# Windowed attention in front of two MoE layers: alternating the column halves in the value products, and one score path for all units

## The chip, the core and the metric

The kernel runs on one core of a Trainium2 chip. The metric is the device time of one execution in microseconds (us), the median of several runs. The engines are TensorE (PE; its weight loads are listed apart as PEld), VectorE (DVE), ScalarE (ACT), GpSimd (POOL) and the DMA queues, most of them issued from SyncE (SP).

## What is computed

Three stages follow each other, all in float32. The change lies in the first.

```
q, k, v: 4 x 8 heads x 576 x 64
scores = 0.125 * q @ k.T ; mask = (rel >= 0) & (rel < 64) ; attn = softmax(where(mask, scores, -1e9))
x  = attn @ v                                   # 2304 tokens x 512
x  = g(x @ w_in) @ w_out                        # 512 -> 2048 -> 512, g piecewise quadratic
out[n] = gate * (relu(x @ w1[e]) @ w2[e])       # e = argmax of x @ w_gate, 8 experts
```

## The kernel before

The 2304 tokens are 18 tiles of 128 rows. Attention is cut into 36 **units**: one tile and one half of the heads (4 heads). The first MoE layer goes over 7 **blocks** of 256 or 384 tokens in **steps**: one step is 12 matmuls of the first layer into `h` (L486, 256 or 384 columns), an activation on ACT and DVE (`a`, `ghi`, `glo`), and 6 or 9 matmuls of the second layer into `acc` (L528, 512 columns), two steps later. Float32 operands of these layers are split into a high part `hi` and a remainder `lo` and multiplied in a faster 32-bit format (fp32r), three products for one. Then follow 48 steps of the second MoE layer and the tokens left over.

A unit goes through these stages: scores into the PSUM tile `S` (`u_qk`), row maximum (`mask_parts`: `mx` on DVE, `nm` on ACT), exponential on ACT (`u_exp`), normalising (`norm_parts`), transposing (`tr_parts`: by PE into `pt`, from unit `DT0` = 24 on by a DMA transpose), copy to `pb`, products with the values (`av_parts`, L442), and a copy to the block's `xT` as hi and lo. The product with the values takes four heads and two blocks of 64 rows, so eight matmuls of 128 rows by 64 columns. In the trace each is two, as every plain float32 matmul there. `od`, the outermost of the three loops, chooses the half of the array's columns: the first four write output partitions 0 to 63, the last four 64 to 127.

There are two score paths. Units 0 to 14 (`NQ`) are multiplied in plain float32 on tiles of 64 rows by 64 columns, four at a time, and PE adds the mask first with small bf16 matmuls (L310, L316). Units 15 to 35 load twice as much (1280 instead of 640 elements a partition, zero-padded or doubled), `u_split` cuts it into hi and lo on ACT, DVE and POOL (L272 to L284), `u_scores` makes eight matmuls of 128 x 128 by 192 columns (L334), DVE adds the mask in two halves and writes the result to SBUF (L343), and the maximum is read from there (L373).

What sets the order: the first 10 units and the first 22 steps stand in a list written out by hand (`HEAD`). After it, `plan` gives each unit a start slot (two slots to a step) and `STAGES`, `STAGES2` (units 15 to 23) or `STAGES3` (from unit 24) say how many slots later each stage is recorded. A scheduler then places the recorded instructions on each engine by its own estimate of when they are ready; each engine runs its queue in that order. Raw inputs of units from 10 on go through one buffer (`RB` = 1), and the load of unit u+1 is issued behind `u_split(u)`.

Of the kernel before, what the change touches and what calls it, by code (L numbers as in the profile page):

```python
# [19 lines left out]
P = 128  # L20
# [25 lines left out]
ST3 = (-3, -1, 0, 1, 2, 6, 7)  # L46
US_A = (0, 3, 4, 5, 7, 11, 21)
UJ_V = ()
ST2 = (-2, -1, 0, 1, 3, 3, 4)
LEFT = (0, 0)  # L50
RB = 1
# [3 lines left out]
NQ = 15  # L55
MASK_PE = tuple(range(NQ))
# [28 lines left out]
QLO_V = (0, 2, 8, 10, 11, 20, 22, 31, 34, 35)  # L85
KLO_V = (0, 1, 3, 5, 8, 10, 11, 12, 22, 24, 31)
QHI_V = (0, 3, 4, 5, 7, 10, 11, 13, 16, 19, 23, 24, 28, 30, 31)
KHI_V = (1, 4, 5, 7, 8, 9, 10, 15, 20, 26, 29, 30, 32, 34, 35)
# [40 lines left out]
def kernel(  # L129
# [3 lines left out]
    qk: bass.AP,  # L133
# [104 lines left out]
    def u_load(u):  # L238
        if u < len(units):
            b, c, hf = units[u]  # L240
            if u < EARLY:
                r = wp.tile([P, 640], F32, tag="w", name="qqr")
            else:
                r = att.tile([P, 640 if u < NQ else 1280], F32, tag="qk", name="qk", bufs=RB)
            nc.sync.dma_start(r, qq[:, u] if u < NQ else qk[:, u - NQ])
            U.setdefault(u, {})["r"] = r
# [16 lines left out]
    def u_split(u):  # L263
        if u < NQ:
            return
        s = U[u]

        raw = s["r"]
        r = att.tile([P, 2048], F32R, tag="qs", name="qs", bufs=QB)
        q, k, kh = r[:, :512], r[:, 512:1280], r[:, 1280:]  # L270
        if u in QHI_V:
            nc.vector.tensor_copy(q, raw[:, :512])  # L272
        else:
            nc.scalar.activation(q, raw[:, :512], ACTF.Copy)  # L274
        if u in KHI_V:
            nc.vector.tensor_copy(kh, raw[:, 512:])  # L276
        else:
            nc.scalar.activation(kh, raw[:, 512:], ACTF.Copy)
        qeng = nc.vector if u in QLO_V else nc.gpsimd
        keng = nc.vector if u in KLO_V else nc.gpsimd  # L280
        qeng.tensor_tensor(  # L281
            out=q[64:], in0=raw[64:, :512], in1=q[64:].bitcast(F32), op=ALU.subtract
        )
        keng.tensor_tensor(out=k, in0=raw[:, 512:], in1=kh.bitcast(F32), op=ALU.subtract)  # L284
        s.update(qs=q, kk=r[:, 512:].rearrange("p (c h k) -> p h c k", c=2, h=4))

    def u_qk(u):
        s = U[u]
        S2 = None
        if u < min(ALT, NQ) and u % 2:  # L290
            S = [ps.tile([P, 512], F32, tag="acc", name="Sa", bufs=3) for _ in range(2)]
        else:
            S2 = ps.tile([P, 2, 512], F32, tag="S", name="S")
            S = [S2[:, a] for a in range(2)]
        s["S"], s["S2"] = S, S2
        if u < NQ:

            rq, rk = s["r"][:, :2 * P], s["r"][:, 2 * P:]

            pe = u in MASK_PE  # L300
            kind = mask_of(u)
            for pr in range(2):
                outs = [
                    (a, r, slice(64 * a, 64 * a + 64), S[a][64 * r:64 * r + 64, pr * P:pr * P + P])
                    for r in range(2) for a in range(2)
                ]
                if pe:
                    for a, r, rows, o in outs:
                        m = 1 + a if kind == 1 + r else 0
                        mm = nc.tensor.matmul(  # L310
                            o, ib[rows, 64 * a:64 * a + 64], mb[rows, m], start=True, stop=False
                        )
                        if u == BEHIND:
                            tc.keep_in_program_order(mm)
                for a, r, rows, o in outs:
                    nc.tensor.matmul(  # L316
                        o,
                        rq[rows, pr * P + 64 * r:pr * P + 64 * r + 64],
                        rk[rows, pr * 192 + 64 * r:pr * 192 + 64 * r + P],
                        start=not pe, stop=True,  # L320
                    )
            return
        s["sr"] = att.tile([P, 4, P], F32, tag="sr", name="sr", bufs=2)
        u_scores(u, S2)

    def u_scores(u, S2):

        s = U[u]
        sr = s["sr"]
        for a in range(2):  # L330
            for b in range(2):
                h = 2 * a + b
                for c in range(2):
                    nc.tensor.matmul(  # L334
                        S2[:, a, 192 * b:192 * b + 192], s["qs"][:, h * P:h * P + P],
                        s["kk"][:, h, c], start=(c == 0), stop=(c == 1),
                    )
        sv = S2[:, :, :384].rearrange("p a (b k) -> p a b k", b=2)
        so = sr.rearrange("p (a b) k -> p a b k", b=2)
        m = mb[:, mask_of(u)].unsqueeze(1).unsqueeze(1).to_broadcast([P, 2, 2, P])  # L340
        for r in range(2):
            rs, ks = slice(64 * r, 64 * r + 64), slice(64 * r, 64 * r + P)
            nc.vector.tensor_tensor(out=so[rs], in0=sv[rs, :, :, ks], in1=m[rs], op=ALU.add)  # L343

    def mask_parts(u):
        s = U[u]
        sr = s["sr"] if u >= NQ else att.tile([P, 4, P], F32, tag="sr", name="sr", bufs=2)
        mx = att.tile([P, 4], F32, tag="mx", name="mx", bufs=2)
        m = mb[:, mask_of(u)].unsqueeze(1)
        if u >= NQ:  # L350
            pass
        elif s["S2"] is not None:
            sv = s["S2"][:, :, :2 * P].rearrange("p a (b k) -> p a b k", b=2)
            if u in MASK_PE:
                nc.vector.tensor_reduce(
                    out=mx.rearrange("p (b a) -> p a b", a=2), in_=sv, axis=AX.X, op=ALU.max
                )
            else:
                nc.vector.tensor_tensor(
                    out=sr.rearrange("p (b a) k -> p a b k", a=2), in0=sv,  # L360
                    in1=m.unsqueeze(1).to_broadcast([P, 2, 2, P]), op=ALU.add,
                )
        else:
            for a in range(2):
                sv = s["S"][a][:, :2 * P].rearrange("p (b k) -> p b k", b=2)
                if u in MASK_PE:
                    nc.vector.tensor_reduce(out=mx[:, a::2], in_=sv, axis=AX.X, op=ALU.max)
                else:
                    nc.vector.tensor_tensor(
                        out=sr[:, a::2], in0=sv, in1=m.to_broadcast([P, 2, P]), op=ALU.add  # L370
                    )
        if u not in MASK_PE:
            nc.vector.tensor_reduce(out=mx, in_=sr, axis=AX.X, op=ALU.max)  # L373
        yield
        nm = att.tile([P, 4], F32, tag="nm", name="nm", bufs=2)
        nc.scalar.activation(nm, mx, ACTF.Copy, scale=-0.125)
        s.update(sr=sr, nm=nm)
# [3 lines left out]
    def u_exp(u):  # L381
# [3 lines left out]
        for h in range(4):  # L385
            nc.scalar.activation(
                sr[:, h], s["S"][h % 2][:, h // 2 * P:h // 2 * P + P] if u in MASK_PE else sr[:, h],
                ACTF.Exp, scale=0.125,
                bias=s["nm"][:, h:h + 1], accum_out=sm[:, h:h + 1],
            )  # L390
# [41 lines left out]
    def av_parts(u):  # L432
# [4 lines left out]
        for od in range(2):  # L437
            for pr in range(2):
                h = 2 * pr + od
                for blk in range(2):  # L440
                    cs = slice(64 * blk, 64 * blk + 64)
# [32 lines left out]
    STAGES = [(-2, u_split), (0, u_qk), (0, u_mask), (1, u_exp), (2, u_norm), (3, u_tr), (4, u_av)]  # L474
    hl = u_split, u_qk, u_mask, u_exp, u_norm, u_tr, u_av
    STAGES2, STAGES3 = list(zip(ST2, hl)), list(zip(ST3, hl))
# [448 lines left out]
    def plan(us, s0, s1):  # L925
        for i, u in enumerate(us):
            st = s0 + ((s1 - 6 - s0) * i) // max(1, len(us) - 1)
            for off, fn in STAGES if u < NQ else STAGES2 if u < DT0 else STAGES3:
                slots.setdefault(st + off, []).append((fn, (u,)))
# [83 lines left out]
    def run_slot(s):  # L1013
        for fn, a in slots.get(s, []):
            fn(*a)
            if fn is u_split and a[0] + RB >= EARLY:
                u_load(a[0] + RB)
# [43 lines left out]
    for x in HEAD:  # L1061
# [10 lines left out]
        if x == "av9":  # L1072
            u_load(10)
            v_load(10)
# [34 lines left out]
def layout(q, k, v, w_in, w_out, w_gate, w1, w2):  # L1109
# [7 lines left out]
    qq = np.zeros((P, NQ, 2 * P + 2 * 192), np.float32)  # L1117
    qk = np.zeros((P, 2 * NTILE - NQ, 4 * P + 4 * 192), np.float32)
    vv = np.zeros((P, NTILE, 2, 2, 4 * D), np.float32)
    for c in range(NTILE):  # L1120
        for hf in range(2):
# [4 lines left out]
            for r in range(2):  # L1126
                o = slice(D * r, D * r + D)
                if u < NQ:
                    qq[o, u, :2 * P] = a[:, r::2].reshape(D, 2 * P)
                    qq[o, u, 2 * P:] = b[:, r::2].reshape(D, 2 * 192)  # L1130
                else:
                    qk[o, u - NQ, :4 * P] = a.reshape(D, 4 * P)
                    qk[o, u - NQ, 4 * P:] = b.reshape(D, 4 * 192)
# [8 lines left out]
        "qq": qq, "qk": qk, "vv": vv, "wi": wi, "wo": wo, "wg": w_gate.T,  # L1142
# [27 lines left out]
```

## Time and profile before

| | |
|---|---|
| median of 3 runs | 745.62 us (745.48 to 746.74) |
| the profiled execution's own time | 744.77 us |
| its span, first to last instruction | 743.0 us |
| PE busy | 714.0 us (96%) |
| DVE, ACT, POOL busy | 488.7, 418.2, 144.5 us |

Busy times of PE count a matmul from its start to its modelled end, and matmuls overlap, so a busy PE can still be made faster. Starts of matmuls are the firmer numbers: the time between the start of one group and the start of the next is what the group costs the queue.

### The profile page before, as it was taken

The numbers are of one execution on the slowest core, as the hardware profiler recorded it, in microseconds if no ns is written. First come the engines' busy times: TensorE is split into PE (matmuls) and PEld (weight loads), VectorE is DVE, ScalarE is ACT, GpSimd is POOL, SyncE is SP. The second block draws the span as 40 slices with busy tenths as digits, with TensorE's granted clock in tenths as the row PEclk, the third lists the DMA queues.
The fourth block names the chain that finished last, engine by engine and source line by source line (L and its number), as shares of the span: only waits on it lengthen the run. The fifth ranks groups of instructions, "written<-read, shape, count | busy, mean of one in ns | idle before, by whom it ended". The sixth has DMA issues, their size and how long they took to land. (4 is left out here: it accounts for less than half of the span.)

```text
span 743.0 us, 12418 instructions
## 1 busy us (share of the span) xinstructions
PE 714.0 (96%) x4507; PEld 630.6 (85%) x4507; DVE 488.7 (66%) x1093; ACT 418.2 (56%) x1031; POOL 144.5 (19%) x120
## 2 busy tenths in 40 slices
PE   6887999998999999999999999999999999999996
PEld 3776998887889889888988899878898999888985
DVE  6898998246567735874686335787789989652110
ACT  6786776666577757675677435476443415163212
POOL 0021000013341113310320000365121202076000
PEclk9798999999999999999999999999999999999999
DMA  9984101325322523562353402343424233143101
GB/s 330 402 316 122 49 1 58 121 89 181 100 87 86 157 64 75 169 134 79 86 169 66 169 1 97 124 127 94 121 75 110 58 99 93 36 141 122 43 1 54
DMA packets 66691, 83.71 MB, mean 113 GB/s; under 512 B 35672, under 2 KB 41560, under 8 KB 66499
## 3 DMA queue, kind: packets, MB, share of 16 engines
q1 hardware_dynamic: 66466, 82.46, 35.7%
q8 instruction: 36, 0.59, 0.3%
q0 software_dynamic: 160, 0.43, 0.2%
q14 instruction: 29, 0.23, 0.1%
HBM read 60.68 MB, written 14.42 MB: 101 GB/s over the span
## 5 line engine op out<-in xcount | busy, mean ns | idle before, releaser
L486 PE MATMUL h<-xT,wi 128*128 128x384 f32 (+1 forms) x1344 | 230.4, 319 | 3.3 <-DVE a L501 3.1
L486 PEld LDWEIGHTS h<-xT,wi 128*128 128x128 f32 x1344 | 211.7, 191 | 14.3 <-DVE a L501 6.3
L528 PE MATMUL acc<-wo,ghi 128*128 128x512 f32 x576 | 154.6, 397 | 0.0
L528 PEld LDWEIGHTS acc<-wo,ghi 128*128 128x128 f32 x576 | 104.1, 189 | 16.8 <-issue 0.7
L623 DVE CUSTOM_DVE_ANT_0 junk<-xg,wgb 128x512 bf16<-128x512 f32 x144 | 113.1, 785 | 3.2
L486 PE MATMUL h<-xT,we 128*128 128x384 f32 x576 | 110.4, 337 | 2.6 <-DVE glo L518 2.6
L486 PEld LDWEIGHTS h<-xT,we 128*128 128x128 f32 x576 | 102.0, 188 | 8.0 <-DVE glo L518 3.5
L501 DVE SCALAR_TENSOR_TENSOR a<-h,a 128x384 f32<-128x384 f32 (+1 forms) x112 | 55.5, 497 | 66.8 <-ACT a L498 66.0
L528 PE MATMUL acc<-wo,glo 128*128 128x512 f32 x288 | 85.9, 394 | 0.0
L509 DVE TENSOR_TENSOR glo<-a,ghi 128x384 fp32r<-128x384 f32 (+1 forms) x106 | 60.4, 571 | 36.4 <-ACT ghi L507 36.3
L497 ACT ACTIVATE a<-h,half 128x384 f32<-128x384 f32 (+1 forms) x112 | 58.7, 526 | 39.7 <-PE h L486 37.7
L528 PE MATMUL acc<-we,ghi 128*128 128x512 f32 x288 | 78.5, 395 | 0.0
L507 ACT ACTIVATE ghi<-a 128x384 fp32r<-128x384 f32 (+1 forms) x112 | 52.6, 474 | 36.3 <-DVE a L501 35.5
L517 ACT ACTIVATE ghi<-h 128x384 fp32r<-128x384 f32 x48 | 23.2, 483 | 72.3 <-PE h L486 59.5
L528 PEld LDWEIGHTS acc<-wo,glo 128*128 128x128 f32 x288 | 53.5, 188 | 11.9 <-issue 0.2
L518 DVE SCALAR_TENSOR_TENSOR glo<-h,ghi 128x384 fp32r<-128x384 f32 x48 | 26.6, 555 | 53.1 <-ACT ghi L517 53.0
L528 PEld LDWEIGHTS acc<-we,ghi 128*128 128x128 f32 x288 | 53.0, 188 | 8.3 <-ACT y L711 0.3
L498 ACT ACTIVATE a<-a 128x384 f32<-128x384 f32 (+1 forms) x112 | 53.4, 477 | 2.6
L964 POOL TENSOR_TENSOR xT<-xj,xT 128x256 fp32r<-128x256 f32 x36 | 31.3, 878 | 89.2 <-ACT xT L963 89.2
L281 POOL TENSOR_TENSOR qs<-qk,qs 64x512 fp32r<-64x512 f32 x16 | 21.3, 1332 | 122.0 <-ACT qs L274 85.7
L528 PE MATMUL acc<-we,glo 128*128 128x512 f32 x144 | 44.1, 395 | 0.0
L284 POOL TENSOR_TENSOR qs<-qk,qs 128x768 fp32r<-128x768 f32 x18 | 35.1, 1949 | 43.6 <-DVE qs L276 26.9
(162 smaller groups left out, 858.2 us busy)
## 6 DMA issues: line engine op xcount, KB each, us to landing
qk<-in_qk_dram SPq DMA_DIRECT2D x21, 640.0 KB, 4.0
er<-in_w_dram SPq DMA_DIRECT2D x32, 256.0 KB, 2.8
wraw<-in_wi_dram SPq DMA_DIRECT2D x14, 512.0 KB, 7.6
wraw<-in_wo_dram SPq DMA_DIRECT2D x14, 512.0 KB, 7.6
vt<-in_vv_dram SPq DMA_DIRECT2D x26, 256.0 KB, 2.8
xg<-x2s SPq DMA_DIRECT2D x18, 256.0 KB, 2.7
out_dram<-y SPq DMA_DIRECT2D x18, 256.0 KB, 2.1
qqr<-in_qq_dram SPq DMA_DIRECT2D x10, 320.0 KB, 7.0
```

Source lines behind the costliest of these rows:

```text
L284: keng.tensor_tensor(out=k, in0=raw[:, 512:], in1=kh.bitcast(F32), op=ALU.subtract)
L486: nc.tensor.matmul(h[:, :n], w[:, wa, k * P:k * P + P], x[:, xa, k, :n], start=(i == 0), stop=(i == 3 * KD - 1),)
L497: nc.scalar.activation(a[:, :n], h[:, :n], ACTF.Relu, scale=0.5, bias=half[:, 0:1])
L498: nc.scalar.activation(a[:, :n], a[:, :n], ACTF.Square)
L501: nc.vector.scalar_tensor_tensor(out=a[:, :n], in0=h[:, :n], scalar=1.0, in1=a[:, :n], op0=ALU.max, op1=ALU.min)
L507: nc.scalar.activation(hi[:, :n], a[:, :n], ACTF.Copy)
L509: (nc.gpsimd if pool else nc.vector).tensor_tensor(out=lo[:, :n], in0=a[:, :n], in1=hi[:, :n].bitcast(F32), op=ALU.subtract)
L517: nc.scalar.activation(hi[:, :n], h[:, :n], ACTF.Relu)
L518: nc.vector.scalar_tensor_tensor(out=lo[:, :n], in0=h[:, :n], scalar=0.0, in1=hi[:, :n].bitcast(F32), op0=ALU.max, op1=ALU.subtract,)
L528: nc.tensor.matmul(a, ga[:, t * P:t * P + P], w[:, wa], start=(first and j == 0), stop=(last and j == 2),)
L623: tc.keep_in_program_order(nc.vector.tensor_tensor_reduce(out=junk, in0=xg[t], in1=Z["wgb"][:, e], scale=1.0, scalar=0.0, op0=ALU.mult, op ...
L964: (nc.vector if 2 * t + i in PL_V else nc.gpsimd).tensor_tensor(out=lo, in0=r, in1=hi.bitcast(F32), op=ALU.subtract)
```

## The change

The eight products with the values are issued with the column half as the innermost loop, so that neighbours lie in different halves. All 36 units take the score path of the first 15: plain float32 on 64 x 64 tiles, mask by PE, maximum and exponential read from PSUM. `u_split`, `u_scores`, the second input `qk`, the lists that dealt the splits out to engines and `STAGES2` are gone. Units 15 to 23 use `STAGES`. There are two raw buffers of half the size, and the load of unit u+2 is issued behind `u_qk(u)`.

```diff
-RB = 1
+RB = 2
-NQ = 15
-ST2 = (-2, -1, 0, 1, 3, 3, 4)
-ST3 = (-3, -1, 0, 1, 2, 6, 7)
+ST3 = (-1, 0, 1, 2, 6, 7)
...
-                r = att.tile([P, 640 if u < NQ else 1280], F32, tag="qk", name="qk", bufs=RB)
-            nc.sync.dma_start(r, qq[:, u] if u < NQ else qk[:, u - NQ])
+                r = att.tile([P, 640], F32, tag="qk", name="qk", bufs=RB)
+            nc.sync.dma_start(r, qq[:, u])
...
-    def u_split(u):
...
-    def u_scores(u, S2):
...
         av = ps.tile([P, 4, P], F32, tag="h" if alt else "tp", name="av", bufs=2 if alt else 1)
-        for od in range(2):
-            for pr in range(2):
-                h = 2 * pr + od
-                for blk in range(2):
-                    cs = slice(64 * blk, 64 * blk + 64)
+
+        for pr in range(2):
+            for blk in range(2):
+                cs = slice(64 * blk, 64 * blk + 64)
+                for od in range(2):
+                    h = 2 * pr + od
                     nc.tensor.matmul(
                         av[64 * od:64 * od + 64, pr, cs],
...
-    STAGES = [(-2, u_split), (0, u_qk), (0, u_mask), (1, u_exp), (2, u_norm), (3, u_tr), (4, u_av)]
+    STAGES = [(0, u_qk), (0, u_mask), (1, u_exp), (2, u_norm), (3, u_tr), (4, u_av)]
...
-            for off, fn in STAGES if u < NQ else STAGES2 if u < DT0 else STAGES3:
+            for off, fn in STAGES if u < DT0 else STAGES3:
...
-            if fn is u_split and a[0] + RB >= EARLY:
+            if fn is u_qk and a[0] + RB >= EARLY:
                 u_load(a[0] + RB)
...
         if x == "av9":
             u_load(10)
+            u_load(11)
             v_load(10)
```

The scheduler's order on PE after the list by hand differs. Here is unit 24 on PE, the transpose of an earlier unit and steps of the third and fourth blocks around it; the last seven of unit 24's score matmuls are the `S<-qs` row, the first stands 72 big matmuls ahead:

```order
L528 MATMUL acc<-wo,glo 128x512
L424 MATMUL pt<-ct,sr 128x128 x4
L528 MATMUL acc<-wo,glo 128x512
L486 MATMUL h<-xT,wi 128x256 x12
L528 MATMUL acc<-wo,ghi 128x512 x4
L528 MATMUL acc<-wo,glo 128x512 x2
L334 MATMUL S<-qs 128x192 x7
```

And the same unit after the change, from the last of its first four mask matmuls (`cb` holds the mask and an identity, `S<-qk` are the scores):

```order
L275 LDWEIGHTS cb
L275 MATMUL S<-cb 64x128
L413 MATMUL h<-xT,wi 128x256 x12
L455 MATMUL acc<-wo,ghi 128x512 x4
L455 MATMUL acc<-wo,glo 128x512 x2
L281 MATMUL S<-qk 64x128 x4
L275 LDWEIGHTS cb
L275 MATMUL S<-cb 64x128
```

Four mask matmuls now stand alone, 18 big matmuls ahead of the rest of the unit's scores. In the same way the scores of units 17 to 24 each stand in two pieces with 128-column work between them.

The second place is a unit of the fifth block's time (384 columns), before:

```order
L528 MATMUL acc<-wo,ghi 128x512 x6
L528 MATMUL acc<-wo,glo 128x512 x3
L334 MATMUL S<-qs 128x192 x8
L486 MATMUL h<-xT,wi 128x384 x3
L442 MATMUL av<-pb,vt 64x64 x8
L486 MATMUL h<-xT,wi 128x384 x9
```

and after:

```order
L455 MATMUL acc<-wo,ghi 128x512 x6
L455 MATMUL acc<-wo,glo 128x512 x3
L370 MATMUL av<-pb,vt 64x64 x8
L275 LDWEIGHTS cb
L275 MATMUL S<-cb 64x128
```

The products with the values and the next scores, which had three `h` matmuls between them, now follow each other directly (the rest of the 16 score rows comes behind, then `h` 12 times). This stands so for five units (units 16 and 26 to 29).

## Rows read from the trace of the kernel before

**Rows 1.** Stretches: length, PE, PEld, DVE, ACT, POOL busy, granted clock, DMA

```profile
0.00:66.50 66.50, 50.66 (x553) 39.94 (x554) 53.90 (x112) 48.14 (x157) 8.92 (x13) 0.85 0.85 312
66.50:135.70 69.20, 69.20 (x358) 62.71 (x356) 60.56 (x109) 47.24 (x88) 0.00 (x0) 1.00 0.13 43
135.70:430.00 294.30, 291.69 (x2086) 259.75 (x2085) 180.35 (x363) 194.93 (x536) 59.51 (x37) 1.00 0.40 116
```

**Rows 2.** Waits of PE, 100 to 430 us: total, times, longest

```profile
PE av L442 <- ACT pb L427: 1.3, 1, 1.3
PE h L486 <- DVE a L501: 1.2, 3, 0.5
```

**Rows 3.** PE in order of time, 329 to 343 us: start, length, what

```profile
334.29 2.27 PE L486 MATMUL h<-xT,wi 128*128 128x384 f32 x12
336.39 1.55 PE L528 MATMUL acc<-wo,ghi 128*128 128x512 f32 x6
337.78 0.86 PE L528 MATMUL acc<-wo,glo 128*128 128x512 f32 x3
338.57 0.97 PE L442 MATMUL av<-pb,vt 128*64 128x64 f32 x16
339.46 2.35 PE L486 MATMUL h<-xT,wi 128*128 128x384 f32 x12
341.66 1.55 PE L528 MATMUL acc<-wo,ghi 128*128 128x512 f32 x6
```

**Rows 4.** Products with the values: instants of 0.01 us, (x) matmuls in flight

```profile
148.69:148.70 0.01, 0.01 (x4) 1.00 0.00 0
148.89:148.90 0.01, 0.01 (x7) 1.00 0.00 0
```

**Rows 5.** The value products as one tile: duration min/median/max in ns

```profile
L442 PE MATMUL av<-pb,vt x416: 222/222/270, 148.4 to 419.2; 128*64 128x64 f32 x139
```

**Rows 6.** Scores: instants of 0.01 us, a unit below 15, a unit above

```profile
149.45:149.46 0.01, 0.01 (x8) 1.00 0.00 0
174.80:174.81 0.01, 0.01 (x2) 1.00 0.00 0
```

**Rows 7.** PE in order of time, 134 to 138 us

```profile
135.75 0.25 PE L310 MATMUL S<-cb 64*64 64x128 bf16 x4
135.83 0.39 PE L316 MATMUL S<-qk 64*64 64x128 f32 x8
136.10 0.39 PE L316 MATMUL S<-qk 64*64 64x128 f32 x8
136.42 1.67 PE L528 MATMUL acc<-wo,ghi 128*128 128x512 f32 x6
137.93 0.39 PE L528 MATMUL acc<-wo,glo 128*128 128x512 f32 x1
```

**Rows 8.** PE in order of time, 184 to 187 us

```profile
184.01 1.04 PE L334 MATMUL S<-qs 128*128 128x192 f32 x8
184.88 1.11 PE L528 MATMUL acc<-wo,ghi 128*128 128x512 f32 x4
```

**Rows 9.** PE in order of time, 148 to 151 us (scores between the first two)

```profile
148.41 0.97 PE L442 MATMUL av<-pb,vt 128*64 128x64 f32 x16
...
149.99 0.73 PE L528 MATMUL acc<-wo,glo 128*128 128x512 f32 x2
150.56 0.52 PE L486 MATMUL h<-xT,wi 128*128 128x256 f32 x3
```

**Rows 10.** ACT and PE in order of time around 179 us, [idle before <- releaser]

```profile
178.16 0.84 ACT L278 ACTIVATE qs<-qk 128x768 fp32r<-128x768 f32 x1 [1.40 <-DMA qk<-in_qk_dram]
...
179.54 0.97 PE L442 MATMUL av<-pb,vt 128*64 128x64 f32 x16 [1.25 <-ACT pb L427]
```

**Rows 11.** Groups by line: busy us, mean ns of one, idle before

```profile
L343 DVE TENSOR_TENSOR sr<-S,cb 64x512 f32<-64x512 f32 x42 | 28.8, 686 | 1.5 <-PE S L334 1.0
```

**Rows 12.** PE in order of time, 61 us

```profile
60.85 1.08 PE L424 MATMUL pt<-ct,sr 128*128 128x128 f32 x4 [2.47 <-DVE xT L456]
```

More of the change, by code (lines that the diff above doesn't have):

```diff
@@ L54 @@
 ALT = 4
-NQ = 15
-MASK_PE = tuple(range(NQ))
 GLO_P = tuple(range(6))
@@ L84 @@
 NORM_P = 14
[L85 to L88, printed above, removed]
 WARM = 10
@@ L132 @@
     qq: bass.AP,
-    qk: bass.AP,
     vv: bass.AP,
@@ L261, in mask_of @@
         return 1 if P * c % SEQ == 0 else 2 if (P * c + 64) % SEQ == 0 else 0
-    def u_split(u):
[L264 to L285, printed above, removed]
     def u_qk(u):
@@ L289, in u_qk @@
         S2 = None
-        if u < min(ALT, NQ) and u % 2:
+        if u < ALT and u % 2:
             S = [ps.tile([P, 512], F32, tag="acc", name="Sa", bufs=3) for _ in range(2)]
@@ L295, in u_qk @@
         s["S"], s["S2"] = S, S2
[L296 to L301, printed above, removed]
-            for pr in range(2):
[L303 to L322, printed above, removed]
@@ L323, in u_qk @@
-        s["sr"] = att.tile([P, 4, P], F32, tag="sr", name="sr", bufs=2)
-        u_scores(u, S2)
-    def u_scores(u, S2):
[L328 to L343, printed above, removed]
+        rq, rk = s["r"][:, :2 * P], s["r"][:, 2 * P:]
@@ new lines, in u_qk @@
+        kind = mask_of(u)
+        for pr in range(2):
+            outs = [
+                (a, r, slice(64 * a, 64 * a + 64), S[a][64 * r:64 * r + 64, pr * P:pr * P + P])
+                for r in range(2) for a in range(2)
+            ]
+            for a, r, rows, o in outs:
+                m = 1 + a if kind == 1 + r else 0
+                mm = nc.tensor.matmul(
+                    o, ib[rows, 64 * a:64 * a + 64], mb[rows, m], start=True, stop=False
+                )
+                if u == BEHIND:
+                    tc.keep_in_program_order(mm)
+            for a, r, rows, o in outs:
+                nc.tensor.matmul(
+                    o,
+                    rq[rows, pr * P + 64 * r:pr * P + 64 * r + 64],
+                    rk[rows, pr * 192 + 64 * r:pr * 192 + 64 * r + P],
+                    start=False, stop=True,
+                )
@@ L345, in mask_parts @@
     def mask_parts(u):
         s = U[u]
-        sr = s["sr"] if u >= NQ else att.tile([P, 4, P], F32, tag="sr", name="sr", bufs=2)
+        s["sr"] = att.tile([P, 4, P], F32, tag="sr", name="sr", bufs=2)
         mx = att.tile([P, 4], F32, tag="mx", name="mx", bufs=2)
[L349 to L362, printed above, removed]
+        if s["S2"] is not None:
+            nc.vector.tensor_reduce(
+                out=mx.rearrange("p (b a) -> p a b", a=2),
+                in_=s["S2"][:, :, :2 * P].rearrange("p a (b k) -> p a b k", b=2),
+                axis=AX.X, op=ALU.max,
+            )
@@ L365, in mask_parts @@
                 sv = s["S"][a][:, :2 * P].rearrange("p (b k) -> p b k", b=2)
[L366 to L373, printed above, removed]
+                nc.vector.tensor_reduce(out=mx[:, a::2], in_=sv, axis=AX.X, op=ALU.max)
         yield
@@ L376, in mask_parts @@
         nc.scalar.activation(nm, mx, ACTF.Copy, scale=-0.125)
-        s.update(sr=sr, nm=nm)
+        s["nm"] = nm
     u_mask = whole(mask_parts)
@@ L386, in u_exp @@
             nc.scalar.activation(
-                sr[:, h], s["S"][h % 2][:, h // 2 * P:h // 2 * P + P] if u in MASK_PE else sr[:, h],
-                ACTF.Exp, scale=0.125,
+                sr[:, h], s["S"][h % 2][:, h // 2 * P:h // 2 * P + P], ACTF.Exp, scale=0.125,
                 bias=s["nm"][:, h:h + 1], accum_out=sm[:, h:h + 1],
@@ L436, in av_parts @@
         av = ps.tile([P, 4, P], F32, tag="h" if alt else "tp", name="av", bufs=2 if alt else 1)
-        for od in range(2):
-            for pr in range(2):
-                h = 2 * pr + od
-                for blk in range(2):
-                    cs = slice(64 * blk, 64 * blk + 64)
+        for pr in range(2):
+            for blk in range(2):
+                cs = slice(64 * blk, 64 * blk + 64)
+                for od in range(2):
+                    h = 2 * pr + od
                     nc.tensor.matmul(
@@ L472, in unit_parts @@
         yield
-    STAGES = [(-2, u_split), (0, u_qk), (0, u_mask), (1, u_exp), (2, u_norm), (3, u_tr), (4, u_av)]
-    hl = u_split, u_qk, u_mask, u_exp, u_norm, u_tr, u_av
-    STAGES2, STAGES3 = list(zip(ST2, hl)), list(zip(ST3, hl))
+    STAGES = [(0, u_qk), (0, u_mask), (1, u_exp), (2, u_norm), (3, u_tr), (4, u_av)]
+    STAGES3 = list(zip(ST3, (u_qk, u_mask, u_exp, u_norm, u_tr, u_av)))
     PASS = ((0, 0), (1, 0), (0, 1))
@@ L1116, in layout @@
     vf = np.concatenate([pad, tok(v)])
-    qq = np.zeros((P, NQ, 2 * P + 2 * 192), np.float32)
-    qk = np.zeros((P, 2 * NTILE - NQ, 4 * P + 4 * 192), np.float32)
+    qq = np.zeros((P, 2 * NTILE, 2 * P + 2 * 192), np.float32)
     vv = np.zeros((P, NTILE, 2, 2, 4 * D), np.float32)
@@ L1127, in layout @@
                 o = slice(D * r, D * r + D)
[L1128 to L1133, printed above, removed]
+                qq[o, u, :2 * P] = a[:, r::2].reshape(D, 2 * P)
+                qq[o, u, 2 * P:] = b[:, r::2].reshape(D, 2 * 192)
             for blk in range(2):
@@ L1141, in layout @@
     return {
-        "qq": qq, "qk": qk, "vv": vv, "wi": wi, "wo": wo, "wg": w_gate.T,
+        "qq": qq, "vv": vv, "wi": wi, "wo": wo, "wg": w_gate.T,
         "w1": a1, "w2": a2, "cst": constants(), "msk": mask_constants(),
```

## The prediction

> **What bounds the kernel now.** I read the stretches first [rows 1]. From 66.5 us on PE never pauses for long: it is busy in all of 69.2 us and then in 291.7 of 294.3 us, at full granted clock, while in the second of these stretches DVE has 180 and ACT 195 us of work. So from 66.5 us to the end of attention at about 430 us the length is that of PE's queue, and a microsecond taken from PE there is a microsecond of the kernel. The waits of PE between 100 and 430 us come to 2.5 us in four pieces [rows 2]. Before 66.5 us it is different: PE is busy in 50.7 of 66.5 us, DVE in 53.9, DMA engines have 85% of the time, and PE waits for ACT and DVE in turn, as in [rows 12], 2.47 us at one transpose. The last stretch, from 430 us on, holds no attention, and no edit moves work there; I expect it to shift as a whole.
>
> 26 of the 36 units (10 to 35) have their products with the values, and 21 (15 to 35) their changed scores, in the stretch that PE bounds. The other ten stand in the list by hand, where PE waits.
>
> **Products with the values.** One isolated burst of 16 takes 0.89 us from its first start to the next group's start (338.57 to 339.46 in [rows 3]). Entering it costs 0.09 us (three `glo` matmuls ahead of it take 0.79 us, at 0.232 each, from 1.39 us for six, they would take 0.70), leaving it 0.10 us (the next twelve `h` take 2.20 against 2.10 us). Together 1.08 us. What of it can shrink? Early in such a burst four matmuls are in flight, later seven [rows 4]; each lasts 222 ns [rows 5]. Four in flight at 222 ns is one start every 56 ns, seven is one every 32 ns. The faster part is where the first half's last products and the second half's first products run beside each other: already now PE takes the second half's ahead of its turn, a few at a time. Unpaired, 16 starts take 16 x 0.056 = 0.89 us; the burst as it stands takes 0.89 less about 0.17 that the last one needs to hand over (0.222 less 0.056, an estimate), so some 0.73 us. Paired throughout, eight starts in each half take 8 x 0.056 = 0.45 us. The saving is 0.28 us a unit, 26 x 0.28 = 7.3 us. Bounds: pairing at the seven in flight that the rows show instead of eight, 16 x 0.032 = 0.51, gives 0.22 a unit and 5.7 us; no pairing at all loses what there is now, 0.89 against 0.73, +0.16 a unit, +4.2 us. I take 7.3, because the scores of the units below 15 do just this already: their plain float32 matmuls, also two in the trace for one in the code, go round four tiles, and eight are in flight where a 192-column score has two [rows 6].
>
> The row shows weight loads and products of two column halves overlapping. [...]
>
> **Scores.** An old score of eight matmuls costs 0.87 us (184.01 to 184.88, [rows 8]), with nothing lost on either side: it is in the same 128 x 128 form as its neighbours. A new one lasts 0.67 us (135.75 to 136.42, [rows 7]), enters with 0.09 (taken from the products) and leaves with 0.12 (six `acc` take 1.51 instead of 1.39 us), 0.88 us. So the exchange itself brings PE nothing: +0.01 x 21 = +0.2 us. But the new form has a price per entry. One round of four masks and four scores lasts 0.27 us (135.83 to 136.10), two 0.55, so 0.33 of the 0.88 us is fixed, and each time the scheduler cuts a unit in two with 128-column work between, that is paid again. By the order after the change this is so for eight units (17 to 24): 8 x 0.33 = +2.6 us. Cutting an old score cost nothing. In five units products and scores now follow each other without 128-column work between. Such a pair lasts 1.58 us (148.41 to 149.99, [rows 9]) plus 0.09 and 0.11 at its ends (two `glo` take 0.57, not 0.46), 1.78, against 1.08 + 0.88 apart: -0.18 each, -0.9 us. Two units have their scores on both sides of a burst of products; I price these at nothing. Sum for the scores +1.9 us, between -0.7 (cuts free) and +3.
>
> **What leaves the other engines.** DVE loses 42 mask adds of 686 ns, 28.8 us [rows 11], and all engines the splits; the maximum stays. These engines have slack, so this is worth only what PE waits for them. The largest wait of the stretch is 1.25 us for `pb` at 179.54: ACT had stood 1.40 us at the split of a raw input whose DMA had not landed, with the copy to `pb` queued behind it [rows 10]. No instruction of ACT or DVE waits for that DMA any more; PE does, but with two buffers the load is out two units ahead. Of the 2.5 us [rows 2] I take 2.0 as gone; bounds 0 and 2.5. The exponential now reads PSUM, so `S` is held until it is done; with one `S` and units four or more slots apart that hides under the steps between. If it did not, the next unit's mask matmuls would stand in PE's queue and everything behind them.
>
> **The chain of units 15 to 23** has three slots from scores to transpose instead of four. A slot is half a step, about 1.4 us (an estimate: six `acc` 1.39 us, twelve `h` of 256 columns two thirds of 2.10, halved). The chain loses the two mask adds, 2 x 0.686 = 1.37 us. The two cancel; nothing is priced.
>
> **The list by hand.** Ten bursts get 0.28 us shorter, but PE waits there for ACT and DVE, and DVE is busy in 81% of the time; only the bursts directly on the way to the next copy count. I take three of ten, -0.8 us, between 0 and -3 (all ten, some at half clock).
>
> **Sum.** -7.3 + 1.9 - 2.0 - 0.8 = -8.2 us. The profiled execution took 744.77 us, 743.0 of it span, and would come to 736.6; the median lies 0.85 us higher. 745.6 - 8.2 = **737.4 us**.
>
> **Rivals.**
> 1. *Waits move* (0.15): units 15 to 23 wait on PE at their transposes, since ACT still needs four exponentials between maximum and sum and the slots are fewer. For it: each unit's chain is only just covered. Against it: units 10 to 13 run in these slots now and [rows 2] has no wait at a transpose. Half a microsecond for nine units, and no old wait gone: -7.3 + 1.9 - 0.8 + 4.5 = -1.7, 743.9 us.
> 2. *The halves do not pair* (0.07): a weight load of one half isn't hidden behind the other half's product, so that alternating even loses the pairing at the hand-over. Then +4.2 + 1.9 - 2.0 = +4.1, 749.7 us, slower. It decides as soon as a burst does not get shorter than its 0.73 us, for the scores and the waits cancel by themselves. Against it: seven and eight in flight [rows 4, 6]. [...]
> 3. *Cuts cost nothing and all waits go* (0.14): -7.3 - 0.7 - 2.5 - 1.5 = -12.0, 733.6 us. For it: a part of the fixed 0.33 us may hide behind the matmul ahead.
> 4. *The change has no effect on the time* (0.05): PE's time comes back as waits for `a`, because a step's activations set the pace. Against it: ACT and DVE are two thirds busy and less here. 745.6 us.
>
> **Numbers.** The forecast has 0.59 with its own range 734.5 to 740. 80% lie between 732.5 and 743: that takes in rival 3 and most of 1 and leaves out 2 and 4. About 0.2% (1.5 us) can be told from no change. Forecast, rival 3 and most of rival 1 are faster, 0.87; rival 4 and a little of 1 the same, 0.06; rival 2 slower, 0.07.
>
> **What would show it.** A burst of products of about 0.6 us from first start to the next group instead of 0.89, with eight in flight all along; scores of 0.67 us; 0.2 to 0.4 us lost at each cut; no wait of ACT for a raw input; PE's wait for `pb` near 179 us gone; the stretch from 430 us on unchanged in length. The prediction is wrong if PE shows new waits at `pt`, `av` or at the masks, if the bursts keep four in flight, or if the stretches of half clock before 66.5 us shift by some us with the altered pattern of work.

## The result and the profile after

The changed kernel takes 734.25 us (median of 4 runs, 733.59 to 735.58) against 746.18 us for the kernel before beside it (745.48 to 748.68): ratio 0.985 with a 95% interval of 0.983 to 0.988, which is 9 to 13 us less. In a second comparison on another occasion it was 734.79 us, ratio 0.984 (0.982 to 0.986). The forecast was 737.4 us, -8.2 us, with an own range of 734.5 to 740 us; the measured time lies just below that range and inside the 80% (732.5 to 743).

The profiled execution has a span of 733.8 us, 9.2 us less. The stretches below are those of [rows 1], moved to nearly the same places in the program: the third begins 1.1 us and ends 0.4 us closer in, so that against it stand 292.8 us of the 294.3 before (length, then busy time of PE, PEld, DVE, ACT, POOL, granted clock, DMA):

```profile
0.00:66.50 66.50, 47.69 (x554) 36.87 (x555) 54.39 (x112) 48.23 (x157) 8.46 (x13) 0.84 0.86 318
66.50:137.90 71.40, 71.40 (x383) 64.77 (x382) 60.68 (x109) 48.66 (x90) 0.00 (x0) 0.98 0.13 41
137.90:422.00 284.10, 283.92 (x2393) 243.43 (x2392) 128.86 (x298) 180.34 (x507) 3.13 (x3) 1.00 0.33 95
422.00:733.80 311.80, 302.39 (x1519) 268.92 (x1517) 194.24 (x511) 128.60 (x250) 76.92 (x70) 1.00 0.29 83
```

The fourth row stands against 313.0 us before. The third row is the one that pays: PE is busy in 283.92 of 284.10 us. DVE has lost some 50 us of work there, POOL all but three instructions. The waits of PE from 100 to 420 us, in [rows 2] two rows with 2.5 us, are one row (total, times, longest):

```profile
PE h L413 <- DVE a L428: 0.2, 1, 0.2
```

An isolated burst of products with the values, beside [rows 3] (start, length, what):

```profile
331.17 1.55 PE L455 MATMUL acc<-wo,ghi 128*128 128x512 f32 x6
332.56 0.86 PE L455 MATMUL acc<-wo,glo 128*128 128x512 f32 x3
333.35 0.69 PE L370 MATMUL av<-pb,vt 128*64 128x64 f32 x16
333.96 2.37 PE L413 MATMUL h<-xT,wi 128*128 128x384 f32 x12
336.17 1.55 PE L455 MATMUL acc<-wo,ghi 128*128 128x512 f32 x6
```

From 333.35 to 333.96 it is 0.61 us, where it was 0.89. Entering and leaving cost what they did (0.79 us for the three `glo`, 2.21 for the twelve `h`). And the number in flight at instants of that burst, beside [rows 4]:

```profile
333.55:333.56 0.01, 0.01 (x6) 1.00 0.00 0
333.65:333.66 0.01, 0.01 (x8) 1.00 0.00 0
333.85:333.86 0.01, 0.01 (x8) 1.00 0.00 0
```

Eight all along after the start: both halves run side by side through the whole burst. That count uses modelled ends; the starts say the same. The 16 matmuls of this burst start in eight pairs, some 58 ns from pair to pair behind the first and 7 ns within one. In the burst of [rows 3] the first half's eight starts stand 58 ns apart behind the first, the second half's likewise, and only the last three of the one run beside the first three of the other.

To see where the time went I count the matmuls of the MoE layers (`h` and `acc`, 3216 in every kernel here) and take the starts of the 461st, the 721st and the 1781st. The first two lie early in attention's part behind the list by hand (at 136.8 and 195.2 us before), the third at its end (429.6). The time between them is PE's alone, whatever was busy in name:

```
us between starts of MoE matmuls  to 461st  461 to 721  721 to 1781  461 to 1781  1781st to the end
before                              136.8        58.5        234.3        292.8        313.4
changed                             137.9        55.3        228.8        284.2        311.8
changed, second profile             135.9        55.6        228.8        284.4        312.0
av_only                             137.0        57.9        231.0        288.9        314.6
scores_only                         137.3        56.7        234.3        291.0        311.8
runs_of_two                         136.9        55.9        229.7        285.6        312.0
scores_whole                        137.1        55.7        225.8        281.5        313.5
scores_whole, second profile        137.2        55.7        225.8        281.5        312.9
one_raw_buffer                      139.4        55.3        228.8        284.1        311.8
raw_once                            136.1        63.4        232.3        295.7        313.2
raw_once_alt                        135.7        64.9        225.7        290.6        313.6
split_once_alt                      137.4        56.3        226.5        282.7        316.1
no_add_alt                          136.0        60.0        230.0        290.0        314.8
no_pool_alt                         136.6        62.5        225.2        287.8        315.8
```

So the change gained 8.6 us between the 461st and the 1781st, lost 1.1 ahead of that and gained 1.6 behind it. In the two kernels that were profiled twice, the column from the 461st to the 1781st repeats within 0.3 us, the first moves by up to 2.0 us and the last by up to 0.6. The last one lies between 311.8 and 316.1 us over all kernels, though no edit touches what it covers. The medians differ by 1 to 3 us more than these profiles do; the spread of the runs (745.48 to 748.68 us before) is as large.

### The profile page after: what moved, and what is told of

Its sections match the earlier page's. It is cut to its first block, busy times and chain, and to the rows that moved or that the text cites. A ratio compares the mean times of both kernels' runs of the same rounds, so it can differ in the third digit from the quotient of the medians.

```text
span 733.8 us, 12894 instructions
## 1 busy us (share of the span) xinstructions
PE 705.4 (96%) x4843; PEld 614.0 (84%) x4843; DVE 438.2 (60%) x1028; ACT 405.8 (55%) x1004; POOL 88.5 (12%) x86
## 5 line engine op out<-in xcount | busy, mean ns | idle before, releaser
L424 ACT ACTIVATE a<-h,half 128x384 f32<-128x384 f32 (+1 forms) x112 | 59.6, 534 | 60.8 <-PE h L413 58.8
L436 DVE TENSOR_TENSOR glo<-a,ghi 128x384 fp32r<-128x384 f32 (+1 forms) x106 | 57.9, 547 | 38.3 <-ACT ghi L434 38.1
L624 POOL TENSOR_TENSOR we<-er,we 128x512 fp32r<-128x512 f32 x16 | 23.5, 1472 | 312.9 <-PE h L413 300.7
L314 ACT ACTIVATE sr<-S,nm 128x128 f32<-128x128 f32 x136 | 48.2, 367 | 1.2
```

The costliest lines, as they stand in the source:

```text
L314: nc.scalar.activation(sr[:, h], s["S"][h % 2][:, h // 2 * P:h // 2 * P + P], ACTF.Exp, scale=0.125, bias=s["nm"][:, h:h + 1], accum_out=s ...
L424: nc.scalar.activation(a[:, :n], h[:, :n], ACTF.Relu, scale=0.5, bias=half[:, 0:1])
L436: (nc.gpsimd if pool else nc.vector).tensor_tensor(out=lo[:, :n], in0=a[:, :n], in1=hi[:, :n].bitcast(F32), op=ALU.subtract)
L624: nc.gpsimd.tensor_tensor(out=w[:, 1], in0=raw, in1=w[:, 0].bitcast(F32), op=ALU.subtract)
```

## The experiments

**The two halves of the change alone, and with whole score units.** Each is a kernel of its own: the kernel before with only the new loop order in `av_parts`; the changed kernel with the old loop order; and the changed kernel with every mask and score matmul of units 15 to 35 pinned behind what was recorded ahead of it on PE:

```diff
+PIN = tuple(range(15, 36))
...
                 if u == BEHIND or u in PIN:
                     tc.keep_in_program_order(mm)
...
+                if u in PIN:
+                    tc.keep_in_program_order(mm)
```

> The kernel before with the products alternating between halves, nothing else. Theory A (PE sets the pace, each burst is 0.28 us shorter, and the old scores' waits are a separate matter): a burst of 0.62 us to the next group's start, 26 x 0.28 = 7.3 us less, 739 us against 746, ratio 0.990; PE still waits 1.3 us for pb near 179 us and about 2.5 us in all between 100 and 430 us. Rival B (the gain came from ACT and DVE having less to do, and a shorter burst only turns into waits): 743 us or more, and PE's waits in that stretch grow to 6 us or more.

Measured 742.65 us, ratio 0.996 (0.993 to 0.998), near the border of rival B's 743 and 3.7 us off theory A's 739. The bursts did get as short as in the changed kernel, 26 times 0.28 us, 7.3 us. But the stretch shrank by 3.9 us alone. The rest turned into waits (total, times, longest, 130 to 425 us):

```profile
PE h L487 <- DVE a L502: 3.6, 6, 1.0
PE av L443 <- ACT pb L427: 1.3, 1, 1.3
PE S L310 <- ACT sr L386: 0.3, 1, 0.3
```

Before there were three waits for `a`, 1.2 us [rows 2]. My theory A was wrong in that the two parts add up; rival B has about half of it.

> The changed kernel with the products in the old order of halves: only the score path is changed. Theory A (the scores gain about 3.9 us of waits on PE and lose 2.6 us to cut units): 743 to 745 us, ratio 0.996 to 0.998, bursts of 0.89 us, PE waits below 0.5 us between 100 and 420 us. Rival B (the lighter ACT and DVE carry the change): 739 us or less, ratio 0.991 or less.

Measured 740.97 us, ratio 0.993 (0.991 to 0.995), between the two. In the stretch it gained 1.8 us, where theory A has 3.9 - 2.6 = 1.3, and PE waits for nothing in it; the rest lies in the last column, which I come back to. The two halves of the change give 3.9 + 1.8 = 5.7 us in the stretch, together they give 8.6. The lighter score path is what lets the shorter bursts through: on it they shorten the stretch from 291.0 to 284.2 us, 6.8 of their 7.3 us.

> The changed kernel with the 16 mask and score matmuls of each unit from 15 on pinned behind what was recorded ahead of them on PE, so that nearly no unit is cut by 128-column work. Theory A (each cut costs PE 0.3 to 0.5 us and nothing pays it back): about 3 us less than the changed kernel, 731 us, ratio to before 0.980. Rival B (the cuts filled time in which PE would have waited, or the later scores make the exponential and the transposes late): 734 us or more, with new waits at the transposes or the products.

Measured 733.35 us, ratio 0.983 (0.981 to 0.985), and beside the changed kernel 733.55 against 734.79 us:

> The changed kernel once more, beside the next run on one chip: 734 us.

> The changed kernel with whole score units, beside the changed kernel on one chip. If cutting the units costs what PE's starts show up to the end of attention (2.6 us), 731.5 us, 2 to 3 us less than the changed kernel; if the last stretch gives it back, within 1 us of it.

Ratios 0.982 (0.980 to 0.985) and 0.984 (0.982 to 0.986). The stretch is 2.6 to 2.9 us shorter, as theory A asks, with a single wait in it (0.8 us for `a` at 178 us). The whole time is 1.2 us less, inside the intervals and between the two forecasts: the last column is 0.9 to 1.7 us longer, and the first moves by itself. So uncut units are worth 2.6 us or more on PE; that the kernel as a whole is faster by it isn't shown.

**How far ahead PE starts the other half.** The loops in `av_parts` were set to `pr`, `od`, `blk`, so that the half changes after two products.

> The changed kernel with the halves changing after every two products of the code (four matmuls in the trace) instead of after every one. Theory A (PE starts the other half's matmuls several places ahead of their turn, as it did at the one change of half before): nearly all pair, bursts of 0.62 to 0.70 us to the next group, 734 to 736 us. Rival C (only neighbours in different halves pair): bursts of 0.80 us or more, 738 us or more.

Measured 736.1 us, ratio 0.987 (0.984 to 0.990). A burst takes 0.66 us to the next group, within theory A's 0.62 to 0.70:

```profile
333.56 0.73 PE L370 MATMUL av<-pb,vt 128*64 128x64 f32 x16
334.22 2.35 PE L413 MATMUL h<-xT,wi 128*128 128x384 f32 x12
```

With its ends it costs 0.86 us by PE's starts, against 0.81 when the half changes every time and 1.09 when it changes once. Theory A: neighbours need not be in different halves, the other half's matmuls start some places early. With runs of eight in the trace three pairs were found, with runs of four nearly all.

**What made PE wait on the old score path.** The first idea was the transfer of the raw input, from [rows 10].

```diff
     def u_load(u):
         if u < len(units):
             b, c, hf = units[u]
+            if u > NQ:
+                U.setdefault(u, {})["r"] = once[0]
+                return
...
+            if u == NQ:
+                once.append(r)
```

> The kernel before, in which units 16 to 35 don't load their raw inputs: their splits read the raw input of unit 15, so that no split waits for a transfer; all split work stays. The scheduler's order shifts a little with it. Theory D (PE's 3.9 us of waits come from ACT and DVE standing at a split whose raw input has not landed): about 4 us less, 742 us or below, PE's starts between 137 us and the end of attention closed up, ACT without waits at the splits. Rival E (they come from the split work itself, which fills ACT and DVE at the wrong moment): no change within 1 us, and the waits of PE stay.

> The same with the products alternating between halves: the old score path with all its work, units 16 to 35 splitting the raw input of unit 15. Theory D (late raw inputs took back half of the shorter bursts): 736 us or less, ratio 0.988 or less, waits of PE below 1 us between 130 and 425 us. Rival E (the split work takes it back): within 2 us of the run that only alternates, 740 us or more.

Measured 748.52 us, ratio 1.005 (1.003 to 1.008), and 743.46 us, 0.998 (0.996 to 1.000). By the total, theory D fails, and I took it to have failed. The stretches of the second of them say otherwise (length, PE, PEld, DVE, ACT, POOL busy, granted clock, DMA):

```profile
137.00:171.00 34.00, 32.97 (x320) 27.67 (x320) 15.96 (x37) 25.01 (x82) 6.14 (x5) 1.00 0.38 127
171.00:200.60 29.60, 26.78 (x188) 24.10 (x187) 21.21 (x40) 18.57 (x57) 13.21 (x9) 0.83 0.19 63
200.60:426.30 225.70, 225.70 (x1550) 202.10 (x1550) 145.65 (x286) 151.95 (x394) 39.83 (x24) 1.00 0.24 65
```

From 200.6 us on PE waits for nothing: 225.7 us against 231.0 in the run that only alternates. Before that it loses 7 (64.9 us from the 461st to the 721st start, against 57.9). In the order that the scheduler made here, the scores of two units stand close together on PE, and the second waited 1.6 us for DVE to read the first out of `S`; behind a wait of 0.7 us at 172 and beside this one the granted clock, 0.83 on average over these 29.6 us, was at half for 10 us in all. So in this run the later waits are gone, and at the entry there is a new one. The edit changed both the inputs and the order, and the run doesn't part the two.

```diff
-RB = 2
+RB = 1
...
-            u_load(11)
```

> The changed kernel with one raw buffer instead of two (each of the smaller size), loads issued one unit ahead. Theory D in its strict form (it is the lead of the load that matters): waits of PE at the scores for the raw input, 1 us or more at several units, 737 us or more. Rival F (it matters that ACT and DVE have nothing to wait for and that PE frees the buffer right after the scores): no change, within 1 us of the changed kernel.

Measured 734.9 us, ratio 0.986 (0.983 to 0.989), the stretch 284.1 us: no difference. On the new path a load one unit ahead is early enough, since nothing holds the buffer once PE has read it. The second buffer buys nothing here.

**Splits or mask adds.** In the first kernel `u_split` returns unit 15's result for all later units, so that the later raw loads are gone with the splits; in the second the two adds of `u_scores` are left out and maximum and exponential read `S`.

> Alternating products on the old score path, with the hi/lo split done once, for unit 15; units 16 to 35 multiply unit 15's split inputs, and neither load nor split their own. The mask adds on DVE stay. Theory G (the splits on ACT, DVE and POOL are what makes step activations late and takes back half of the shorter bursts): PE's lost time between 130 us and the end of attention falls by 3 us or more against the run that only alternates, 737 us or less. Theory H (the two mask adds on DVE in each unit's chain do it): the waits stay, 740 us or more.

> Alternating products on the old score path, without the mask adds of units 15 to 35 (the mask is left out; maximum and exponential read PSUM); the splits stay. Theory H: 737 us or less, the stretch to the end of attention 3 us or more shorter than in the run that only alternates. Theory G: the waits stay, 740 us or more.

Measured 737.17 us, ratio 0.987 (0.984 to 0.989), and 742.55 us, 0.994 (0.992 to 0.997). Without the splits the stretch is 282.7 us, 6.2 shorter than in the run that only alternates, with one wait of 0.7 us for `a` in it, at 171 us. Without the adds it is 290.0. By the totals theory G holds and theory H fails, although DVE lost over 20 us of work in either case. But H doesn't fail by its waits. Read by stages, as above, the waits of PE behind 196 us are these, first in the run that only alternates, then without the adds:

```profile
PE h L487 <- DVE a L502: 2.3, 4, 1.0
```

```profile
PE S L334 <- issue: 0.2, 1, 0.2
PE pt L422 <- DVE sr L398: 0.2, 1, 0.2
```

No wait for `a` is left there; by PE's starts some 1 us is lost there, against some 4. What the run gives back, it gives back in other places. At the entry two waits come close together:

```profile
PE av L441 <- ACT pb L425: 1.6, 1, 1.6
PE S L334 <- POOL qs L284: 1.6, 1, 1.6
```

And the scheduler's new order cuts two bursts of products into three pieces each, which by PE's starts cost 1.6 us a burst instead of 0.81, here the first:

```profile
285.56 0.33 PE L441 MATMUL av<-pb,vt 128*64 128x64 f32 x2
...
288.82 0.33 PE L441 MATMUL av<-pb,vt 128*64 128x64 f32 x2
...
292.77 0.57 PE L441 MATMUL av<-pb,vt 128*64 128x64 f32 x12
```

So taking out the splits clears PE's later waits, and so, nearly, does taking out the adds. These two runs don't decide between G and H.

**POOL's part.** In the run that only alternates, this stands around the longest wait for `a`, at 313.5 us (start, length, engine):

```profile
311.48 1.03 PE L334 MATMUL S<-qs 128*128 128x192 f32 x8
313.47 2.35 PE L487 MATMUL h<-xT,wi 128*128 128x384 f32 x12 [0.96 <-DVE a L502]
...
310.55 1.68 DVE L276 CAST qs<-qk 128x768 fp32r<-128x768 f32 x1
312.15 0.68 DVE L180 COPY pp<-sr 128x1024 uint16<-128x1024 uint16 x1
312.86 0.56 DVE L502 SCALAR_TENSOR_TENSOR a<-h,a 128x384 f32<-128x384 f32 x1
...
310.51 1.30 POOL L281 TENSOR_TENSOR qs<-qk,qs 64x512 fp32r<-64x512 f32 x1 [7.78 <-ACT qs L274]
```

The cast on DVE lasts 1.68 us, its kind 0.56: it begins with POOL's subtraction and ends only after it, and `a`, for which PE waits, stands two places behind it. Counted over all instructions of DVE from 137 to 420 us, 14 last over 0.2 us longer than the median of their kind, 12.6 us together (12.8 before, none in the changed kernel). The longest but one is a normalising multiply, its kind 0.69 us, beside another of POOL's subtractions:

```profile
240.61 2.18 DVE L400 TENSOR_TENSOR sr<-sr,rc 128x512 f32<-128x512 f32 x1
...
240.41 1.84 POOL L284 TENSOR_TENSOR qs<-qk,qs 128x768 fp32r<-128x768 f32 x1
```

```diff
-QLO_V = (0, 2, 8, 10, 11, 20, 22, 31, 34, 35)
-KLO_V = (0, 1, 3, 5, 8, 10, 11, 12, 22, 24, 31)
+QLO_V = tuple(range(36))
+KLO_V = tuple(range(36))
```

> Alternating products on the old score path, all of it computed, with the 34 subtractions of the split that ran on POOL moved to DVE (37 with three that end early are on POOL in that stretch before). In the run that only alternates, 14 DVE instructions last longer than their kind by 12.6 us in all, each beside a POOL instruction (a normalising multiply 2.18 instead of 0.69 us), and several of the step activations that PE waits for stand behind them. Theory J (DVE standing still while POOL works is what takes back the shorter bursts): DVE gets some 28 us more work, yet no such long instructions remain, and the stretch to the end of attention is 3 us or more shorter than in the run that only alternates (288.9 us), 738 us or less. Theory K (it is the amount of split work on ACT and DVE): 28 us more on DVE makes PE wait more, 742 us or more.

Measured 741.78 us, ratio 0.994 (0.992 to 0.996): by the total theory J fails. None of the long instructions is left, and with 27 us of subtractions more on DVE the column from the 721st on is 225.2 us, the shortest of all, with no wait of PE behind 190 us. That half is as J says and against K. But such instructions alone don't make PE wait either: behind 200 us the run without late inputs has 14 of them, 10.9 us, the run without the adds 13, 14.6 us, and PE's waits there are gone in both but for 0.4 us. And here the early part is 4.6 us longer, mainly from one place (PE in order of time, then a stretch with its clock):

```profile
178.15 1.11 PE L334 MATMUL S<-qs 128*128 128x192 f32 x8 [1.06 <-DVE qs L281]
179.19 0.69 PE L443 MATMUL av<-pb,vt 128*64 128x64 f32 x16
181.86 1.44 PE L487 MATMUL h<-xT,wi 128*128 128x256 f32 x5 [1.99 <-DVE a L502]
```

```profile
130.00:180.60 50.60, 48.51 (x462) 41.52 (x460) 25.18 (x57) 32.70 (x105) 3.12 (x3) 1.00 0.36 111
180.60:187.40 6.80, 5.54 (x25) 5.54 (x26) 6.29 (x14) 4.75 (x17) 0.00 (x0) 0.50 0.80 267
```

The subtractions and the end of the first half of a block met on DVE, PE stood for 3 us in two waits close together, and from 180.6 us, during the second, the granted clock was 0.50 for 6.8 us.

## Why the prediction was right, point by point

**The number.** The profiles are 9.2 and 10.7 us shorter than the one before, where -8.2 was forecast. In the first, -7.3 for the products, +2.6 for the scores and -3.9 for the waits make the -8.6 of the stretch; +1.1 ahead of it and -1.6 behind it make the rest. The mechanisms of the first three are the forecast's own. That the sum came so near also rests on errors of opposite sign, and the last stretch was not foreseen.

**Bound.** Right: PE loses 0.2 us to waits in its stretch, and what its queue saved there came off the time, once nothing else stood in the way.

**Products with the values.** -7.3 us forecast, 26 x 0.28 = 7.3 measured, eight in flight, as the scores had promised, and a burst of 0.61 us against 0.89. The forecast reads weight loads out of [rows 4], which count matmuls alone; in the trace of the burst of [rows 3] the loads of 138 ns start some 58 ns apart, beside matmuls of their own half, and in the burst of 0.61 us they start in pairs as the matmuls do, some 58 ns from pair to pair and 7 ns within one. But the forecast counted these 7.3 us as a term that stands by itself. Alone it is worth 3.9 us of the stretch, because on the old score path some 3.4 come back as waits (7.3 us lost by PE's starts, 3.9 before). It was right only in company.

**Scores.** +1.9 us forecast, +2.6 measured, with the same mechanism. The isolated exchange costs nothing (0.88 against 0.89 us), five pairs that follow each other save 0.15 us each on average (0.19 where the products come first, nothing for the one unit where they come second). Mis-sized was the cut: 0.33 us forecast, 0.30 to 0.55 measured, about 3.5 us for eight instead of 2.6. Two units show the difference, the first unit 17, cut inside a round of four tiles:

```profile
185.29 0.62 PE L455 MATMUL acc<-wo,glo 128*128 128x512 f32 x2
185.84 0.25 PE L275 MATMUL S<-cb 64*64 64x128 bf16 x4
185.92 0.39 PE L281 MATMUL S<-qk 64*64 64x128 f32 x6
186.24 1.22 PE L413 MATMUL h<-xT,wi 128*128 128x256 f32 x8
...
198.36 0.32 PE L281 MATMUL S<-qk 64*64 64x128 f32 x1
...
199.00 1.20 PE L455 MATMUL acc<-wo,ghi 128*128 128x512 f32 x4
```

The first piece costs 0.40 us and 0.19 at its ends, the second 0.64 and 0.19, 1.42 in all instead of 0.88. Unit 24, cut between masks and scores, the first piece alone:

```profile
275.89 0.62 PE L455 MATMUL acc<-wo,glo 128*128 128x512 f32 x2
276.44 0.25 PE L275 MATMUL S<-cb 64*64 64x128 bf16 x4
276.62 1.69 PE L413 MATMUL h<-xT,wi 128*128 128x256 f32 x12
```

0.18 us and 0.19 at its ends, 0.37; with the second piece 1.22. So the cut through a round costs 0.54 us more than a whole unit, the one between masks and scores 0.34; why the first costs more, no run tests. I had priced only the entry. That cuts cost PE time is shown by the kernel with whole units, 2.6 to 2.9 us shorter in the stretch.

**Waits.** -2.0 us forecast, about -3.9 measured (8.6 = 7.3 - 2.6 + 3.9): the largest error in the sum. I read the waits from the idle time of PE, 2.5 us [rows 2]. A busy time with modelled ends hides the first part of each wait; by starts of matmuls the same places had lost 3.9: at 222.06 us, say, the idle time is 0.43 us and the next `h` starts 0.68 late. The cause I gave, ACT standing at a late raw input, is one link of it. The others that the runs point to are the splits behind the late inputs on ACT, DVE and POOL, the DVE instructions that last longer beside POOL's (12.8 us before), and the mask adds, all in the queues in which the steps' activations wait. Taking out the splits, only the late inputs, only POOL's share or only the mask adds leaves PE with 0, 0, 0 and 0.4 us of idle time behind 196 us, against 2.3 where the products merely alternate. So easing any one of these links nearly clears the waits. Each of these edits also changed the scheduler's order, so that a chance meeting of instructions in one order isn't excluded; and three of the four runs had a pile-up of their own at the entry. Which share each link has in the kernel before stays open.

**The chain of units 15 to 23** with a slot less: right, no wait at a transpose.

**The list by hand.** -0.8 us forecast, +1.1 in the first profile and -0.9 in the second. In the first the granted clock was 0.50 from 59.0 to 69.2 us instead of from 59.6 to 66.5. No gain is shown, and none can be told apart from these 3 us more at half clock.

**The last stretch** was to stay as it is. It is 1.3 to 1.6 us shorter in all five profiles with the changed order, against the one profile before. PE's waits there, first before the change from 430 us, then after from 422:

```profile
PE h L486 <- DVE glo L518: 2.6, 2, 1.4
PE h L486 <- DVE a L501: 1.9, 3, 0.9
```

```profile
PE h L413 <- DVE glo L445: 1.5, 2, 1.3
PE h L413 <- DVE a L428: 1.7, 3, 0.7
```

It is mainly one wait near 560 us, 1.2 before and 0.3 after, for `glo` on DVE, whose input `ghi` on ACT stood behind a copy of a transposed tile. It varies from kernel to kernel (1.5 us in the kernel with whole units, and longest in the run without splits, 316.1 us), and no run took it apart. What sets it is open.

Rival 1 did not come about; rival 2 is excluded for this kernel by the bursts of 0.61 us with eight in flight; of rival 3 the waits came true and the free cuts did not. Rival 4, PE's time coming back as waits for `a`, failed for the whole change, but with the products alone about half of it came true.

## What to carry to other kernels

Count what a group of matmuls costs from start to next start, ends included, and count how many are in flight: here four to seven became eight and a burst of 0.89 us became 0.61, while PE's busy share was 96% before and after. The small tiles cost here what the large ones did (0.88 against 0.89 us a unit) where the scheduler left a unit whole, and 0.30 to 0.55 us more where it cut one; look at its order before pricing them. And the shorter bursts on the engine that sets the pace paid only as far as the engines behind it kept up, 3.9 of 7.3 us on the old score path: try both halves of a change alone, since here 3.9 and 1.8 us made 8.6. A run that takes work away also gets a new order from a scheduler, which can hide what it gained: read it by stages, not by its total alone.

## What the runs showed of the hardware that was not expected

- In the burst of [rows 3], where the half changes once in 16, PE does not start the matmuls strictly in the order of the program: the second half's first one starts when five of the first half's eight have started. With runs of four nearly all pair (with its ends a burst costs 0.86 us, against 0.81 when the half changes every time). Which half a matmul belongs to is read from the two trains of starts, 58 ns apart; the trace doesn't name it.
- A unit of 64 x 64 tiles that is cut in two by 128-column work costs PE 0.30 to 0.55 us more than a whole one of 0.88, in the eight cut units of the changed kernel.
- In the run that only alternates 14 DVE instructions last over 0.2 us longer than their kind, 12.6 us in all, such as a cast of 1.68 instead of 0.56 us and a normalising multiply of 2.18 instead of 0.69. POOL's subtractions began 0.04 and 0.20 us ahead of these two and ended 0.42 and 0.54 us before them. In the kernel before, all 14 (12.8 us) begin while a subtraction of POOL's runs and end 0.03 to 0.55 us after it. None is left in the changed kernel or where the subtractions run on DVE. The busy time of neither engine shows it as a wait.
- In the run with the subtractions on DVE, PE waited 1.1 and 2.0 us within 5 us, and from 180.6 us, during the second wait, the granted clock was 0.50 for 6.8 us; in the 50.6 us ahead of that stretch and in the 62.6 us behind it was at 1.00.
